# Banded attention and a feed-forward on one core: the score products in eight pieces of 32 queries instead of four of 64

## The chip, the core and the metric

One core of one Trainium2 chip runs the whole kernel. The metric is the device time of one execution in microseconds (us); lower is better.

## The reference

Four batches, eight heads, 768 positions, head dimension 64. Each query sees the 8 global keys and the 96 latest positions with itself; scores carry a per-head linear bias by distance. The attention output, 3072 tokens of 512, then goes through a gated feed-forward without activation.

```python
scores = scale * np.matmul(q, k.transpose(0, 1, 3, 2))
keep = is_global | ((rel >= 0) & (rel < n_local))        # 8 global, 96 local
scores = np.where(keep, scores + bias, -1e9)
a = softmax(scores)
x = np.matmul(a, v)                                      # then (B*S, H*D)
out = ((x @ w1) * (x @ w2) @ w3) @ w_out
```

## The kernel before, in words

Queries are worked in chunks of 256 (`T`), twelve chunks in all (`NC`), three per batch. A chunk has four pairs of heads (`NP`); a step `s` takes two pairs of one chunk, so there are 24 steps. The two heads `u` of a pair lie on the two halves of the partitions (rows 0 to 63 and 64 to 127), so a product of one head contracts 64 rows.

`scores(c, hp, qr)` (from L408) makes the scores of one pair of heads. For each of the two blocks `j` of 128 queries, for each half `g` of 64 queries (`HQ`) and each head `u`, one matmul (L419) takes 64 queries as weights and streams the keys that these 64 queries can see: 96 window keys, 8 global keys and the own ones, cut to columns g*64 to g*64+167 of the 232 (`UW`), 168 columns. Its output stands on 64 of the 128 partitions of a PSUM bank; each head `u` has a bank of its own (`ps[u]`). So four products (two halves by two heads) sit on four different 64x64 quarters of the array. The first block of a batch has no window before it (`w0 = BW` cuts the first 104 columns): its halves stream 64 and 128 columns. The data are plain float32; the profile has two matmul and two weight-load records for each such product.

`rows` (L434, L435) takes the scores from PSUM: VectorE adds the bias and finds the maximum, ScalarE exponentiates. `values` (L522) makes attention times V, also in 64x64 quarters (rows 64 or 40, 64 columns of weights, 64 or 128 columns streamed). The probabilities come back transposed through DRAM (`swap`, L484; `back`, L493) and are used two steps later.

The order of TensorE's work is written out by hand. From step 5 on, `visit(s, sv, True)` issues for step `s`: the scores of the first pair, half of the products of `values` of step s-2, the scores of the second pair, the other half of `values`. Then `slices` issues a run of the feed-forward (L172 to L174, L192 to L194: 128x128 weights, 512 or 256 streamed columns, in a one-pass float32 format), 72 matmuls long, until the next visit. Steps 0 to 3 (`first_visit`) issue half of `values`, both scores, the other half, between matmuls that fold w3 and w_out (L153); step 0 has no `values`, and step 4 has scores alone. After the 24 steps come two visits of `values` alone (128 or 104 rows of weights, 64 columns) and the rest of the feed-forward.

Of the kernel before, what the change touches and what calls it, by code (L numbers as in the profile page):

```python
# [20 lines left out]
P = 128  # L21
# [7 lines left out]
BK = 32  # L29
NB = P // BK  # L30
# [3 lines left out]
SLOT = GLB + P  # L34
KW = WIN + NQ * SLOT
BW = WIN + GLB
# [5 lines left out]
HQ = P // 2  # L42
# [296 lines left out]
def banded(ctx, tc, ff, ns, nt, nf, oki, ident, qk, vx):  # L339


    nc = tc.nc
# [64 lines left out]
    def scores(c, hp, qr):  # L407

        ps = sc[hp % STEP]
        for j in range(NQ):
            w0 = BW if c % NCB == 0 and j == 0 else 0
            for g in range(P // HQ):
                cols = slice(max(w0, g * HQ), BW + (g + 1) * HQ)
                q0 = KW + j * P + g * HQ
                for u in range(2):
                    m = qr[u * D:(u + 1) * D]
                    nc.tensor.matmul(ps[u][g * HQ:(g + 1) * HQ, j, cols], lhsT=m[:, q0:q0 + HQ], rhs=m[:, j * SLOT:][:, cols], start=True, stop=True)  # L419
        return ps  # L420

    def rows(c, hp, ps):
# [138 lines left out]
    def visit(s, sv, ahead):  # L561


        uu = None if sv is None else spread(sv)
        ps = [None, None]

        def some(i):
            ps[i] = scores(*pairs(s)[i], qrs[s][i])

        def half(k):  # L570
            if uu is not None:
                if k:
                    nc.scalar.activation(uu[:, :, T], ident[:, :STEP], AF.Copy)
                values(uu, sv, k)

        if ahead:
            some(0)
        half(0)
        if not ahead:
            some(0)  # L580
        some(1)
        half(1)
        return ps, uu
# [157 lines left out]
    with tc.manual_schedule(engines={mybir.EngineType.PE}):  # L741
        with tc.manual_schedule(engines={mybir.EngineType.DVE, mybir.EngineType.SP}):
            first_steps()
        with tc.manual_schedule(engines={mybir.EngineType.Activation, mybir.EngineType.SP}):
            for s in range(SWAP + 1, n):
                sv = s - 2 if s > SWAP + 1 else None
                ps, uu = visit(s, sv, True)
# [66 lines left out]
```

## Time and profile before

| | |
|---|---|
| median of 3 runs | 553.4 us (550.91 to 554.24) |
| the profiled execution, its own time | 552.61 us |
| its span in the trace | 550.8 us (1.8 us lie around it) |
| TensorE (PE) busy | 529.9 us, 96% of the span |
| VectorE, ScalarE busy | 308.8 us, 241.7 us |
| matmul records | 4232, of which L419 has 768 and L522 1376 |
| granted TensorE clock, mean | 0.994 |

The profile is of one execution. A matmul's record has its start; its end is modelled, so the time that one takes from the next is read from the distance of two starts and not from its duration. The merged timeline puts neighbouring instructions of one line and operation into one row with their count; the row's shape is that of the first of them. A short window of the timeline shows the instructions that lie in it, so the first start in such a row tells one group of matmuls from the next.

### The profile page before, as it was taken

The page shows a single profiled execution, that of the slowest core. Times are in us where ns is not written, and L with a number is a line of the kernel's source. Part 1 is how long each engine was busy: PE and PEld are TensorE (multiplying, and loading weights), DVE is VectorE, ACT ScalarE, POOL GpSimd, SP SyncE. Part 2 cuts the span into 40 slices and gives each one's busy share as a digit, 9 for nine tenths or more (in the row PEclk, how much of TensorE's full clock was granted, in tenths as well). Part 3 has the DMA queues.
Part 4 walks back from the last instruction along what each step waited for, and adds up shares of the span by engine and source line. Part 5 has one row for each costly group of instructions (what it writes and reads, how often), then busy time and mean ns, then how long its engine had stood idle before and what let it go on. Part 6 is the DMA issues. An engine that isn't in the chain of part 4 may idle for free.

```text
span 550.8 us, 10912 instructions
## 1 busy us (share of the span) xinstructions
PE 529.9 (96%) x4232; PEld 422.5 (77%) x4232; DVE 308.8 (56%) x930; ACT 241.7 (44%) x713; POOL 4.7 (1%) x22
## 2 busy tenths in 40 slices
PE   2999999999898999999999999999999999999995
PEld 0445559989886888888888888888888888888884
DVE  8999999976575457525655544565266551023200
ACT  3065687565465346415643553454265341122210
POOL 0000000000000000000000000000000000000000
PEclk9999999999899999999999999999999999999998
DMA  8897556769999676478547765864784475100011
GB/s 294 308 355 286 192 206 239 200 228 260 228 234 252 164 221 167 147 205 242 135 145 194 187 210 150 231 142 149 225 236 137 126 202 129 52 1 0 0 40 43
DMA packets 47420, 98.64 MB, mean 179 GB/s; under 512 B 3968, under 2 KB 27520, under 8 KB 47360
## 3 DMA queue, kind: packets, MB, share of 16 engines
q1 hardware_dynamic: 47360, 97.86, 59.7%
q8 instruction: 35, 0.57, 0.4%
q14 instruction: 25, 0.20, 0.1%
HBM read 69.54 MB, written 28.31 MB: 178 GB/s over the span
## 4 chain that ended last, share of the span: by engine, by line
PE 86%; DMA 7%; DVE 2%; ACT 2%; SPq 1%; issue 1%; DVEq 0%; ACTq 0%
PE m L172 15%; PE m L174 15%; PE m L173 15%; PE w L153 9%; PE o L192 8%; PE o L193 7%; PE o L194 7%; PE v L522 5%; PE s L419 5%; DMA ph<-d 5%; DMA stage<-w3t 1%; DMA d<-ph 1%; SPq L493 1%; ACT pr L435 1%; DVE pr L434 1%
## 5 line engine op out<-in xcount | busy, mean ns | idle before, releaser
L435 ACT ACTIVATE pr<-pr,mx 128x232 f32<-128x232 f32 (+1 forms) x192 | 88.1, 461 | 26.6 <-DVE mx L434 26.3
L172 PE MATMUL m<-xh,w2h 128*128 128x512 f32 (+1 forms) x224 | 82.1, 367 | 0.0
L181 DVE TENSOR_TENSOR a<-m,a 128x512 f32<-128x512 f32 x48 | 32.9, 685 | 85.8 <-PE m L174 85.6
L173 PE MATMUL m<-xl,w2h 128*128 128x512 f32 (+1 forms) x224 | 80.9, 361 | 0.0
L174 PE MATMUL m<-xh,w2l 128*128 128x512 f32 (+1 forms) x224 | 80.7, 360 | 0.0
L172 PE MATMUL m<-xh,w1h 128*128 128x512 f32 (+1 forms) x224 | 80.6, 360 | 0.0
L174 PE MATMUL m<-xh,w1l 128*128 128x512 f32 (+1 forms) x224 | 80.4, 359 | 0.0
L173 PE MATMUL m<-xl,w1h 128*128 128x512 f32 (+1 forms) x224 | 80.3, 359 | 0.0
L192 PE MATMUL o<-wh,gh 128*128 128x512 f32 x192 | 76.0, 396 | 0.0
L64 ACT ACTIVATE gh<-a 128x512 fp32r<-128x512 f32 x45 | 28.4, 632 | 106.8 <-DVE a L181 106.8
L434 DVE CUSTOM_DVE_ANT_0 pr<-s,biasw 128x232 f32<-128x232 f32 x160 | 53.7, 395 | 38.2 <-PE s L419 38.2
L193 PE MATMUL o<-wl,gh 128*128 128x512 f32 x192 | 74.9, 390 | 0.0
L194 PE MATMUL o<-wh,gl 128*128 128x512 f32 x192 | 74.7, 389 | 0.0
L484 DVE STREAM_TRANSPOSE ph<-pr 128x512 f32<-128x512 f32 x84 | 49.2, 642 | 2.8 <-ACT pr L447 2.3
L153 PE MATMUL w<-wo,t 128*128 128x512 f32 x80 | 39.9, 633 | 9.4 <-DVE wo L59 9.4
L172 PEld LDWEIGHTS m<-xh,w2h 128*128 128x128 f32 x224 | 42.7, 191 | 7.1 <-DVE oki L335 0.2
L174 PEld LDWEIGHTS m<-xh,w2l 128*128 128x128 f32 x224 | 42.7, 191 | 6.4
L179 ACT ACTIVATE a<-m 128x512 f32<-128x512 f32 x48 | 28.5, 593 | 43.5 <-PE m L174 43.5
L173 PEld LDWEIGHTS m<-xl,w2h 128*128 128x128 f32 x224 | 42.7, 191 | 6.0
L172 PEld LDWEIGHTS m<-xh,w1h 128*128 128x128 f32 x224 | 42.3, 189 | 6.4
L174 PEld LDWEIGHTS m<-xh,w1l 128*128 128x128 f32 x224 | 42.3, 189 | 6.4
L173 PEld LDWEIGHTS m<-xl,w1h 128*128 128x128 f32 x224 | 42.3, 189 | 6.3
(93 smaller groups left out, 664.2 us busy)
## 6 DMA issues: line engine op xcount, KB each, us to landing
d<-ph SPq DMA_DIRECT2D x42, 512.0 KB, 5.8
ph<-d SPq DMA_DIRECT2D x84, 256.0 KB, 7.9
qr<-qk SPq DMA_DIRECT2D x16, 624.0 KB, 4.1
vr<-vx SPq DMA_DIRECT2D x17, 512.0 KB, 6.1
stage<-w3t SPq DMA_DIRECT2D x15, 512.0 KB, 6.3
out_dram<-ot SPq DMA_DIRECT2D x24, 256.0 KB, 4.3
raws<-w SPq DMA_DIRECT2D x10, 512.0 KB, 6.2
qr<-qk SPq DMA_DIRECT2D x8, 520.0 KB, 4.6
```

Of the source, the lines that this page charges most:

```text
L153: nc.tensor.matmul(ps, lhsT=self.t3[f, z][:, i * P:(i + 1) * P].bitcast(F32), rhs=self.wo[:, k].bitcast(F32), start=k == 0, stop=k == NFC - 1)
L172: nc.tensor.matmul(ps[:, z], lhsT=mh, rhs=xh[:, i], start=i == 0, stop=False)
L173: nc.tensor.matmul(ps[:, z], lhsT=mh, rhs=xl[:, i], start=False, stop=False)
L174: nc.tensor.matmul(ps[:, z], lhsT=ml, rhs=xh[:, i], start=False, stop=i == NCC - 1)
L179: nc.scalar.activation(a, ps, AF.Copy)
L181: nc.vector.tensor_tensor(out=a, in0=ps, in1=a, op=ALU.mult)
L192: nc.tensor.matmul(ps, lhsT=gh[:, f, ts], rhs=self.wh[:, f], start=f == 0, stop=False)
L193: nc.tensor.matmul(ps, lhsT=gh[:, f, ts], rhs=self.wl[:, f], start=False, stop=False)
L194: nc.tensor.matmul(ps, lhsT=gl[:, f, ts], rhs=self.wh[:, f], start=False, stop=f == NFC - 1)
L434: nc.vector.tensor_tensor_reduce(out=pr[:, j, u, w0:], in0=ps[u][:, j, w0:UW], in1=bias, scale=-SCALE, scalar=3.0e38, op0=ALU.add, op1=ALU ...
L435: nc.scalar.activation(pr[:, j, u, w0:], pr[:, j, u, w0:], AF.Exp, bias=m, scale=-1.0, accum_out=sm[:, j, u:u + 1])
L484: nc.vector.transpose(x[:, k, :, u1 - 4 + u0:u1], units[:, u0:, k0:k0 + P].rearrange("p u (b c) -> p b u c", c=BK))
```

## The change

In `scores` the loop over halves of 64 queries becomes a loop over blocks of 32 queries (`NB` = 4, `BK` = 32). Each product has 32 columns of weights and streams the columns g*32 to g*32+135, 136 of them; in the first block of a batch 32, 64, 96 and 128 columns. The eight products of a block (four blocks by two heads) stand on eight different 64x32 pieces of the array. `values` stays in 64x64 quarters, the feed-forward in the whole array. Nothing else is edited.

```diff
@@ -411,12 +411,12 @@
         ps = sc[hp % STEP]
         for j in range(NQ):
             w0 = BW if c % NCB == 0 and j == 0 else 0
-            for g in range(P // HQ):
-                cols = slice(max(w0, g * HQ), BW + (g + 1) * HQ)
-                q0 = KW + j * P + g * HQ
+            for g in range(NB):
+                rows, q0 = slice(g * BK, (g + 1) * BK), KW + j * P + g * BK
+                cols = slice(max(w0, g * BK), BW + (g + 1) * BK)
                 for u in range(2):
                     m = qr[u * D:(u + 1) * D]
-                    nc.tensor.matmul(ps[u][g * HQ:(g + 1) * HQ, j, cols], lhsT=m[:, q0:q0 + HQ], rhs=m[:, j * SLOT:][:, cols], start=True, stop=True)
+                    nc.tensor.matmul(ps[u][rows, j, cols], lhsT=m[:, q0:q0 + BK], rhs=m[:, j * SLOT:][:, cols], start=True, stop=True)
         return ps
```

On TensorE, in the visit of step 16 (s_103 and s_104 are the banks of the two heads of the first pair, v the output of `values`, o the feed-forward's last product), before:

```order
L194 MATMUL o_0_3187<-wh,gl_2744 128x512
L419 MATMUL s_103<-qr_0_3081 64x168
L419 MATMUL s_104<-qr_0_3081 64x168
L419 MATMUL s_103<-qr_0_3081 64x168
L419 MATMUL s_104<-qr_0_3081 64x168
L419 MATMUL s_103<-qr_0_3081 64x168
L419 MATMUL s_104<-qr_0_3081 64x168
L419 MATMUL s_103<-qr_0_3081 64x168
L419 MATMUL s_104<-qr_0_3081 64x168
L522 MATMUL v_0_3200<-ph_0_2928,vr_0_3083 64x128 x4
```

The same place after, from the second block (j = 1) of the first pair on; eight rows like the first eight stand ahead of it:

```order
L419 MATMUL s_103<-qr_0_3337 32x136
L419 MATMUL s_104<-qr_0_3337 32x136
L419 MATMUL s_103<-qr_0_3337 32x136
L419 MATMUL s_104<-qr_0_3337 32x136
L419 MATMUL s_103<-qr_0_3337 32x136
L419 MATMUL s_104<-qr_0_3337 32x136
L419 MATMUL s_103<-qr_0_3337 32x136
L419 MATMUL s_104<-qr_0_3337 32x136
L522 MATMUL v_0_3456<-ph_0_3168,vr_0_3339 64x128 x4
L522 MATMUL v_0_3456<-ph_0_3168,vr_0_3339 64x64 x4
```

Four products of a block became eight, and the products of `values` that follow them are as they were.

On TensorE, in the visit of step 12, the scores of a batch's first block, before:

```order
L419 MATMUL s_103<-qr_0_2317 64x64
L419 MATMUL s_104<-qr_0_2317 64x64
L419 MATMUL s_103<-qr_0_2317 64x128
L419 MATMUL s_104<-qr_0_2317 64x128
L419 MATMUL s_103<-qr_0_2317 64x168
L419 MATMUL s_104<-qr_0_2317 64x168
```

And after:

```order
L419 MATMUL s_103<-qr_0_2509 32x32
L419 MATMUL s_104<-qr_0_2509 32x32
L419 MATMUL s_103<-qr_0_2509 32x64
L419 MATMUL s_104<-qr_0_2509 32x64
L419 MATMUL s_103<-qr_0_2509 32x96
L419 MATMUL s_104<-qr_0_2509 32x96
L419 MATMUL s_103<-qr_0_2509 32x128
L419 MATMUL s_104<-qr_0_2509 32x128
L419 MATMUL s_103<-qr_0_2509 32x136
```

The longest product of the first block streams 128 columns in both; the others became shorter. On VectorE, ScalarE, GpSimd and SyncE the instructions stand in the order in which they stood.

## Rows read from the trace of the kernel before

**Rows 1.** From the page: the share that each engine is busy (first row), then for TensorE the busy tenths in 40 slices of the span, and the granted TensorE clock in tenths.

```profile
PE 529.9 (96%) x4232; PEld 422.5 (77%) x4232; DVE 308.8 (56%) x930; ACT 241.7 (44%) x713; POOL 4.7 (1%) x22
PE   2999999999898999999999999999999999999995
PEclk9999999999899999999999999999999999999998
```

**Rows 2.** From the page: the chain that ended last, shares of the span by engine.

```profile
PE 86%; DMA 7%; DVE 2%; ACT 2%; SPq 1%; issue 1%; DVEq 0%; ACTq 0%
```

**Rows 3.** Busy time by stage: the stretch, its length, the busy time of PE, PEld, DVE, ACT and POOL with the number of instructions, the granted clock, the DMA share and GB/s.

```profile
25.00:84.00 59.00, 58.73 (x440) 31.01 (x433) 57.21 (x152) 37.23 (x107) 0.00 (x0) 1.00 0.70 250
116.00:176.00 60.00, 55.66 (x720) 50.35 (x720) 37.69 (x146) 33.85 (x117) 1.14 (x4) 0.97 0.92 248
250.00:400.00 150.00, 150.00 (x1254) 124.38 (x1256) 77.15 (x249) 67.50 (x206) 1.13 (x4) 1.00 0.66 184
```

**Rows 4.** TensorE's timeline over the visit of step 16: start in us, time to the last modelled end, line, operation, tiles, shape, count.

```profile
302.60 0.39 PE L193 MATMUL o<-wl,gh 128*128 128x512 f32 x1
302.83 0.39 PE L194 MATMUL o<-wh,gl 128*128 128x512 f32 x1
303.15 0.80 PE L419 MATMUL s<-qr 64*64 64x168 f32 x16
303.77 0.85 PE L522 MATMUL v<-ph,vr 64*64 64x128 f32 x32
304.44 0.76 PE L419 MATMUL s<-qr 64*64 64x168 f32 x16
305.01 0.86 PE L522 MATMUL v<-ph,vr 64*64 64x128 f32 x32
305.80 0.50 PE L192 MATMUL o<-wh,gh 128*128 128x512 f32 x1
306.13 0.40 PE L193 MATMUL o<-wl,gh 128*128 128x512 f32 x1
306.37 0.39 PE L194 MATMUL o<-wh,gl 128*128 128x512 f32 x1
```

**Rows 5.** The same timeline in short windows inside that visit: the first group of four score matmuls (its first one alone, then all four), the second, third and fourth group by the first start of each row, then the last two groups of four 64-column matmuls of `values`.

```profile
303.15 0.35 PE L419 MATMUL s<-qr 64*64 64x168 f32 x1
303.15 0.37 PE L419 MATMUL s<-qr 64*64 64x168 f32 x4
...
303.34 0.61 PE L419 MATMUL s<-qr 64*64 64x168 f32 x12
303.48 0.47 PE L419 MATMUL s<-qr 64*64 64x168 f32 x8
303.62 0.32 PE L419 MATMUL s<-qr 64*64 64x168 f32 x4
...
305.56 0.31 PE L522 MATMUL v<-ph,vr 64*64 64x64 f32 x8
305.62 0.25 PE L522 MATMUL v<-ph,vr 64*64 64x64 f32 x4
```

**Rows 6.** TensorE's timeline at the visit with `values` alone (step 22's values, 128 rows by 64 columns of weights): the matmul ahead of it, the first three groups by the first start of each row, the last group, and the two matmuls behind it.

```profile
455.77 0.39 PE L194 MATMUL o<-wh,gl 128*128 128x512 f32 x1
456.09 0.55 PE L522 MATMUL v<-ph,vr 128*64 128x128 f32 x6
456.25 0.39 PE L522 MATMUL v<-ph,vr 128*64 128x128 f32 x4
456.36 0.39 PE L522 MATMUL v<-ph,vr 128*64 128x128 f32 x4
...
457.79 0.28 PE L522 MATMUL v<-ph,vr 104*64 104x128 f32 x2
458.00 0.50 PE L192 MATMUL o<-wh,gh 128*128 128x512 f32 x1
458.33 0.40 PE L193 MATMUL o<-wl,gh 128*128 128x512 f32 x1
```

**Rows 7.** The timeline of the weight loads (PEld) at the visit of step 16; in brackets the idle time before a row.

```profile
302.61 0.19 PEld L194 LDWEIGHTS o<-wh,gl 128*128 128x128 f32 x1
303.14 0.49 PEld L419 LDWEIGHTS s<-qr 64*64 64x64 f32 x16 [0.35 <-issue]
```

**Rows 8.** Length and busy time of six visits, columns as in Rows 3: steps 0, 3, 4, 16, 12 (scores of a batch's first block) and 14 (values of a batch's first block).

```profile
24.80:25.97 1.17, 1.17 (x34) 0.93 (x33) 1.17 (x4) 0.00 (x0) 0.00 (x0) 1.00 0.22 39
81.46:84.11 2.65, 2.65 (x98) 2.58 (x97) 2.56 (x6) 1.51 (x4) 0.00 (x0) 1.00 0.00 0
104.88:106.18 1.30, 1.30 (x33) 1.06 (x32) 1.23 (x10) 0.60 (x1) 0.00 (x0) 1.00 1.07 212
303.15:305.80 2.65, 2.65 (x98) 2.56 (x97) 1.80 (x11) 1.12 (x6) 0.00 (x0) 1.00 0.03 6
226.97:229.49 2.52, 2.52 (x97) 2.37 (x96) 1.73 (x13) 1.05 (x6) 0.00 (x0) 1.00 0.02 7
265.19:267.60 2.41, 2.41 (x85) 2.31 (x85) 1.56 (x9) 1.59 (x6) 0.00 (x0) 1.00 0.00 0
```

**Rows 9.** TensorE's timeline in the stretch in which it waits for the probabilities' way through DRAM (steps 6 and 8).

```profile
141.20 0.44 PE L522 MATMUL v<-ph,vr 64*64 64x128 f32 x4 [0.22 <-DMA ph<-d]
143.12 0.77 PE L522 MATMUL v<-ph,vr 40*64 40x128 f32 x24 [1.49 <-DMA ph<-d]
...
170.38 0.61 PE L522 MATMUL v<-ph,vr 64*64 64x64 f32 x18 [1.13 <-DMA ph<-d]
```

## The prediction

> **What bounds the kernel now.** I read the page's shares first, then the chain that ended last, then the stages, and then single visits of the timeline. TensorE is busy 96% of the span, and its busy tenths stand at 9 from the second slice nearly to the end; the clock row shows full speed in all slices but one and the last [rows 1]. The chain runs over TensorE for 86% [rows 2]. In the long middle, 250 to 400 us, TensorE is busy 150.00 of 150 us [rows 3]: there, what a visit takes longer or shorter moves the end by as much. Only between 116 and 176 us does it wait, for 4.3 us in all [rows 3].
>
> One visit is the unit of everything below. That of step 16 reads [rows 4]: the last feed-forward matmul starts at 302.83, the first scores at 303.15, values at 303.77, second scores at 304.44, values at 305.01, feed-forward again at 305.80. So a pair's scores take 0.62 and 0.57 us, and the visit 2.65 us [rows 8].
>
> **What streaming costs.** The score matmuls start in groups of four, at 303.15, 303.34, 303.48, 303.62, with values at 303.77 [rows 5, 4]: a pass of 168 columns takes 0.1425 us, and a pair's scores are four passes (two blocks, two records for each product), 0.57 us. Four products are therefore in flight together, since 16 records of 0.14 us in a row would be 2.3 us. A pass of 128 columns takes 0.109 us (456.25 to 456.36 [rows 6]), one of 64 columns 0.056 to 0.06 us (305.56 to 305.62 [rows 5]). Between the first two that is 0.84 ns a column, so 136 columns take 0.109 + 8 x 0.00084 = 0.116 us, if eight products run together as four do now. A pair's scores then stream 4 x 0.116 = 0.463 us: 0.107 us less. In a batch's first block the longest products stream 128 columns and 136 after it, 2 x 0.109 + 2 x 0.116 = 0.45 us against 0.109 x 2 + 0.1425 x 2 = 0.50: 0.05 less. There are 48 pairs, 16 of them with a first block: 32 x 0.107 + 16 x 0.053 = 4.3 us. That is all that the change can bring.
>
> The issue rate seems not to stand against it: the four starts of a group lie within 0.37 - 0.35 = 0.02 us, 7 ns apart [rows 5], so eight start within 0.047 us, less than one pass; and 64-column passes already issue four matmuls and four loads in 0.056 us, 14 ns a pair, which is what eight in 0.116 us need.
>
> **What a change of the array's cut costs.** Feed-forward matmuls start 0.227 us apart (302.60, 302.83), but the first scores start 0.32 us after the last of them: 0.09 us lost [rows 4]. The weight loads show why: the next load could have come one matmul earlier, but starts at 303.14, beside its own matmul, after 0.35 us of idle "issue" [rows 7]. The array runs dry before it is cut anew, and the first load is in the open: the first pass takes 0.19 us instead of 0.1425, 0.05 more for 64 columns of weights. On the way out, the last group starts at 305.62 [rows 5]; the last of its four starts 0.03 later and ends its pass at 305.71; the feed-forward starts at 305.80, again 0.09 later, and its next start is 0.33 behind instead of 0.227: 0.10 more for 128 columns of weights. The visit with 128x64 weights shows the same two prices: 455.77 to 456.09, then 0.16 for the first pass against 0.11; and 457.79 + 0.109 to 458.00, then 0.33 [rows 6]. Between scores and values, both in 64x64 quarters, there is no such loss now (304.44 + 0.57 = 305.01 [rows 4]).
>
> After the change scores stand in 64x32 pieces and values in 64x64 quarters, so a visit has three more changes of cut: scores to values, values to scores, scores to values. No row shows a change between these two cuts. The bounds: 0 at the least, and at the most what 64x64 to 128x128 costs, 0.09 + 0.10 + 0.03 of skew = 0.22 us. The nearest rows are those into 64-wide weights, 0.09 + 0.05; for 32-wide weights I take half the open load, 0.025 us, since 64 cost 0.05 and 128 cost 0.10. I take 0.09 dry, plus 0.05 or 0.025, plus the skew of the last group, since a dry array waits for the last piece: 0.03 for values, 0.047 for eight scores.
>
> The Trainium skill bears on the open point: "TensorEngine Tiling (Array Packing)", Key Properties, says that changing the tiling mode, unlike changing the tile, drains the engine. The trace agrees where the whole array is one side (the 0.09 us above), and no row here shows it between two small cuts. Another of its pages, "TensorE: Matmul & The Clock Gate", Part 3, gives about 4 ns for each further tile; the rows have 7 ns, and the rows decide: by the page the skew of eight would be 0.028 instead of 0.047, about 1 us less over 48 pairs.
>
> **The sum, against the profiled execution (552.6 us; span 550.8).** Visit of step 16: three dry ends +0.28; open loads +0.05 + 0.05 (values), +0.025 (second scores), -0.025 (first scores, 32 wide now) = +0.10; skew 2 x 0.047 + 0.03 = +0.12; streaming -0.21. Together +0.28, 2.65 to 2.93 us. Seven visits are like it (steps 5, 10, 11, 16, 17, 22, 23): +2.0.
>
> Visits whose scores have a first block (6, 7, 12, 13, 18, 19) take 2.52 [rows 8]. Today a quarter that is done early goes on with values; after the change all wait for the 128-column piece. Scores 0.45 + 0.025 + 0.047 + 0.09 = 0.61 each, values 0.67 + 0.05 + 0.02 + 0.09 = 0.83 and 0.79 + 0.04 = 0.83: 2.88, +0.37 each, +2.2 for six. Visits whose values have a first block (8, 9, 14, 15, 20, 21) take 2.41 [rows 8]: 2 x 0.625 for scores, 0.61 and 0.72 for the shorter values make 2.58; with the lags that the present 2.41 also has, between +0.17 and +0.28, I take +0.22: +1.3.
>
> Early steps: step 0 (1.17 us) and step 4 (1.30 us [rows 8]) have two pairs' scores and no values, so no new change of cut: -0.10 and -0.21. Steps 1 to 3 (step 3: 2.65 us [rows 8]) have two new ones against two pairs' saving: +0.1 to +0.2 each, +0.5. Together +0.2. Between 25 and 84 us VectorE is nearly as full (57.21 of 59 us [rows 3]), so this may come out smaller.
>
> In steps 6 to 8 the first values wait for a transfer anyway (1.49 and 1.13 us [rows 9]) and hide the change ahead of them: -0.4. The later ones of these visits are not hidden: loads of the next step go out when the visit has ended.
>
> Sum: 2.0 + 2.2 + 1.3 + 0.2 - 0.4 = 5.3, rounded to 5.5 us for lags as in the last kind of visit. 552.6 + 5.5 = 558.1; the median of the runs shown is 0.8 above the profiled one, so 558.9: I say 559.0 us. VectorE and ScalarE see scores 0.05 earlier or 0.2 later; they wait for TensorE at these points now and have room.
>
> **The rivals.**
> *A. No dry array between the two small cuts.* Pieces of 64x32 would follow quarters of 64x64 as quarters follow one another now. For it: inside a visit nothing is lost between scores and values today, quarters run ahead of one another. Against it: every change of cut that the trace shows is paid, even into 128x64. Then the full 4.3 us come back: 553.4 - 4.3 = 549.1. It decides below 4.3 us over 63 new changes (19 x 3 + 3 x 2), 0.07 us each; from there the change is no longer slower.
> *B. Still only four products at a time.* Eight pieces need four streams of keys from the same 64 partitions instead of two, and no row shows four. If they share what two have, or if two pieces take turns in a quarter, a pair's scores take 8 passes of 0.116, 0.93 us against 0.57: +0.36 x 48 = +17 us, 570 without dry ends and 576 with them. For it: only that the rate of four streams is unseen. Against it: today four loads and four matmuls overlap in two streams a half without loss [rows 5].
> *C. The wait that lowered the clock.* In one slice the granted clock falls [rows 1], in the stage with the 1.49 us wait (mean 0.97 over 60 us [rows 3]), worth 1.8 us. It may come or go with a small shift: +-1.8 us on any case.
>
> **How the numbers follow.** Forecast 0.68 (556 to 563), A 0.18 (547.5 to 551), B 0.14 (568 to 578). A measurement here can tell about 1% from no change, 5.5 us: the forecast's centre lies on that line, so half of it counts as slower (0.36 with its upper tail) and the rest as the same; B is slower; A is within 1% in two of three cases. Slower 0.50, same 0.44, faster 0.06. The range from 549 to 566 leaves out most of B and the lower part of A.
>
> **What would show it.** In the visit of step 16, now at about the same place: score passes of eight starts within 0.05 us, 0.116 us apart (right), or two sets of four (B). Gaps between scores and values: the first values pass 0.05 long, and a start about 0.09 after the last score pass has streamed; PEld idle "issue" not once but four times a visit. Visit length 2.9 us. If it is 2.45 us, A holds; at 3.3 or more, B. L419 shows 1536 matmul records. I am wrong if visits grow and the end does not, or if the difference lies outside the visits.

## The result and the profile after

The changed kernel takes 559.48 us (median of 4, 558.77 to 561.05), the kernel before 553.12 in the runs beside it: ratio 1.0124, 95% interval 1.0085 to 1.0163. The forecast was 559.0. The profiled execution took 559.07 us, its span is 557.3 us, 6.5 more than before.

The busy row of [rows 1] and the row of [rows 2], of the kernel after:

```profile
PE 535.3 (96%) x5000; PEld 419.3 (75%) x5000; DVE 309.8 (56%) x930; ACT 241.6 (43%) x713; POOL 4.7 (1%) x22
PE 86%; DMA 7%; DVE 2%; ACT 2%; SPq 1%; issue 1%; DVEq 0%; ACTq 0%
```

TensorE has 768 more matmul records (1536 of L419 instead of 768) and is busy 5.4 us longer; VectorE and ScalarE are within 1 us of before. Below, "matmuls" with a count are such records, two to a product. The chain runs over it as before.

TensorE's timeline over the visit of step 16, to be laid beside [rows 4]:

```profile
307.05 0.39 PE L194 MATMUL o<-wh,gl 128*128 128x512 f32 x1
307.37 0.69 PE L419 MATMUL s<-qr 64*32 64x136 f32 x32
307.99 0.90 PE L522 MATMUL v<-ph,vr 64*64 64x128 f32 x32
308.82 0.69 PE L419 MATMUL s<-qr 64*32 64x136 f32 x32
309.45 0.90 PE L522 MATMUL v<-ph,vr 40*64 40x128 f32 x32
310.27 0.50 PE L192 MATMUL o<-wh,gh 128*128 128x512 f32 x1
```

From one start to the next: scores 0.62, values 0.83, scores 0.63, values 0.82 us. Values, which nobody edited, were 0.67 and 0.79; the scores, which were to become shorter, are as long as before (0.62) or longer (0.57). Short windows of the same timeline show why, as in [rows 5]: the first of the eight score matmuls and all eight, then the second, third and fourth pass by the first start of each row, then the first two passes of values, the last pass of values and the scores behind it.

```profile
307.37 0.30 PE L419 MATMUL s<-qr 64*32 64x136 f32 x1
307.37 0.35 PE L419 MATMUL s<-qr 64*32 64x136 f32 x8
307.50 0.53 PE L419 MATMUL s<-qr 64*32 64x136 f32 x20
307.62 0.44 PE L419 MATMUL s<-qr 64*32 64x136 f32 x16
307.74 0.32 PE L419 MATMUL s<-qr 64*32 64x136 f32 x8
...
307.99 0.34 PE L522 MATMUL v<-ph,vr 64*64 64x128 f32 x4
308.15 0.41 PE L522 MATMUL v<-ph,vr 64*64 64x128 f32 x12
...
308.65 0.24 PE L522 MATMUL v<-ph,vr 64*64 64x64 f32 x4
308.82 0.33 PE L419 MATMUL s<-qr 64*32 64x136 f32 x6
```

Eight products do run together: eight starts lie within 0.35 - 0.30 = 0.05 us, and the passes follow 0.12 us apart (307.50, 307.62, 307.74). The scores' last pass starts at 307.74, its eighth matmul 0.05 later, and has streamed at 307.74 + 0.05 + 0.116 = 307.90; values start at 307.99, 0.09 later. Their first pass takes 0.16 us (308.15 - 307.99) where 0.109 is usual: 0.05 for loads in the open. The last values start from 308.65 on, 0.06 of pass and 0.03 of skew end at 308.74, and the scores start at 308.82, 0.08 later. The weight loads show the same from their side: the idle "issue" of [rows 7] now also stands ahead of both blocks of values. Ahead of the second scores the loads pause only 0.06 us (307.99 + 0.77 to 308.82), so the view marks three such pauses in the visit, not the four that were to be seen.

```profile
307.36 0.41 PEld L419 LDWEIGHTS s<-qr 64*32 64x32 f32 x32 [0.35 <-issue]
307.99 0.77 PEld L522 LDWEIGHTS v<-ph,vr 64*64 64x64 f32 x32 [0.21 <-issue]
308.82 0.41 PEld L419 LDWEIGHTS s<-qr 64*32 64x32 f32 x32
309.44 0.76 PEld L522 LDWEIGHTS v<-ph,vr 40*64 40x64 f32 x32 [0.21 <-issue]
```

The six visits of [rows 8], in the same order (steps 0, 3, 4, 16, 12, 14):

```profile
24.92:26.00 1.08, 1.08 (x65) 0.87 (x64) 1.08 (x4) 0.00 (x0) 0.00 (x0) 1.00 0.18 19
81.64:84.43 2.79, 2.79 (x130) 2.44 (x129) 2.69 (x6) 1.63 (x4) 0.00 (x0) 1.00 0.02 6
105.09:106.24 1.15, 1.15 (x65) 0.94 (x65) 1.08 (x9) 0.60 (x1) 0.00 (x0) 1.00 1.12 219
307.37:310.27 2.90, 2.90 (x129) 2.35 (x128) 2.03 (x13) 1.31 (x6) 0.00 (x0) 1.00 0.02 6
230.02:232.90 2.88, 2.88 (x129) 2.32 (x128) 1.88 (x13) 1.30 (x7) 0.00 (x0) 1.00 0.02 6
268.89:271.56 2.67, 2.67 (x118) 2.11 (x117) 1.89 (x11) 1.80 (x7) 0.00 (x0) 1.00 0.02 6
```

Where no change of cut was added (steps 0 and 4) the visit is shorter by 0.09 and 0.15 us, although its products doubled; everywhere else it is longer, by 0.14 (step 3), 0.25, 0.36 and 0.26. The 14 visits from step 10 on make 6 x 0.26 + 4 x 0.36 + 4 x 0.26 = 4.0 us (by the starts the visit of step 16 takes 2.905 us, 0.26 more). That is what lies between the start of step 10 (188.59 us before, 191.10 after, the next two rows, the first of before) and the end of the span: 362.2 us before, 366.2 after.

```profile
188.59 0.37 PE L419 MATMUL s<-qr 64*64 64x168 f32 x4
```

```profile
191.10 0.35 PE L419 MATMUL s<-qr 64*32 64x136 f32 x8
```

The other 2.5 us came up before step 10; more on them below.

### The profile page after: what moved, and what is told of

Same layout as the page of the kernel before. It is cut to its first block, busy times and chain, and to the rows that moved or that the text cites. A ratio compares the mean times of both kernels' runs of the same rounds, so it can differ in the third digit from the quotient of the medians.

```text
span 557.3 us, 12448 instructions
## 1 busy us (share of the span) xinstructions
PE 535.3 (96%) x5000; PEld 419.3 (75%) x5000; DVE 309.8 (56%) x930; ACT 241.6 (43%) x713; POOL 4.7 (1%) x22
## 4 chain that ended last, share of the span: by engine, by line
PE 86%; DMA 7%; DVE 2%; ACT 2%; SPq 1%; issue 1%; DVEq 0%; ACTq 0%
PE m L172 15%; PE m L174 14%; PE m L173 14%; PE w L153 8%; PE o L192 7%; PE o L193 7%; PE o L194 7%; PE v L522 7%; PE s L419 5%; DMA ph<-d 5%; DMA d<-ph 2%; DMA stage<-w3t 1%; SPq L493 1%; ACT pr L435 1%; ACT pr L447 1%
```

## The experiments

The theory on trial, D: each change between the 64x32 and the 64x64 cut lets the array run dry and opens the first load. The rival, I: the loss sits in the eighths themselves, in the issue of twice as many products. The table gives the times (n executions, the ratio against the kernel before in the runs beside them) and the length of three visits, taken from the starts in each timeline; it is these that tell the theories apart, since TensorE waits for no other engine in them, but for one wait named below. These lengths are within 0.01 us in two traces of one kernel, while the time scatters: the kernel before took between 550.6 and 557.8 us.

| run | n | median us | ratio, 95% | step 16 | step 12 | step 14 |
|---|---|---|---|---|---|---|
| before, in four sets of runs | 4 to 25 | 552.25 to 553.81 | | 2.65 | 2.52 | 2.41 |
| changed | 4 | 559.48 | 1.0124 (1.0085 to 1.0163) | 2.91 | 2.88 | 2.67 |
| changed, again | 6 | 560.41 | 1.0140 (1.0094 to 1.0187) | 2.91 | 2.88 | 2.67 |
| changed, values first | 10 | 560.31 | 1.0109 (1.0078 to 1.0140) | 2.81 | 2.74 | 2.58 |
| before, values first | 10 | 556.11 | 1.0046 (1.0016 to 1.0077) | 2.65 | 2.51 | 2.41 |
| changed, finer | 4 | 576.44 | 1.0456 (1.0407 to 1.0504) | 3.55 | 3.52 | 3.52 |
| before, finer | 4 | 562.11 | 1.0170 (1.0126 to 1.0213) | 2.88 | 2.81 | 2.70 |
| values in eighths too | 10 | 557.71 | 1.0083 (1.0056 to 1.0110) | 2.85 | 2.78 | 2.44 |
| values in eighths only | 4 | 570.43 | 1.0299 (1.0241 to 1.0357) | 3.42 | 3.29 | 3.03 |
| changed, values first from step 10 | 4 | 559.74 | 1.0122 (1.0079 to 1.0165) | 2.81 | 2.74 | 2.58 |
| the same, again | 12 | 558.69 | 1.0094 (1.0067 to 1.0122) | 2.81 | 2.74 | 2.58 |
| before, last two visits cut up | 1 | 558.51 | | 2.65 | 2.52 | 2.41 |

**One change of cut less.** The order within a visit, from step 5 on, once on the changed kernel and once on the kernel before:

```diff
-                ps, uu = visit(s, sv, True)
+                ps, uu = visit(s, sv, False)
```

> The changed kernel (64x32 scores), but from step 5 on a visit issues half of the values, both pairs' scores, the other half: two new changes of cut a visit instead of three. Theory D (the array runs dry at each change of cut and the first load is in the open): one dry end (0.09), one open load (0.05) and one skew (0.02 to 0.05) less, visit of step 16 about 2.75 us instead of 2.91, 19 visits, about 3 us faster than the changed kernel: 556.5 us, ratio to the kernel before 1.006. Rival I (the loss is in the eighths themselves: issue, loads, skew within a pass): the number of changes does not matter, the time stays at 559.5, ratio 1.012.

> Control: the kernel before (64x64 scores) in the same order, half of the values, both pairs' scores, the other half. No change of cut within a visit in either order. Both theories: visit 2.65 us, time as before, 553 us within 0.3%; if the order itself brings something (a later start of the scores, an earlier need of the probabilities), it is seen here and is taken off the other run.

In the visit the change of cut shows, 0.09 to 0.14 us less for one change, while the control's visits stay within 0.01 us. It is not the whole 0.16 that theory D had: both pairs' scores now stand in one block of 64 matmuls, and that block is 0.06 longer than two of 32 without their dry end (rows below, 310.40 to 311.55).

```profile
310.40 1.22 PE L419 MATMUL s<-qr 64*32 64x136 f32 x64
311.55 0.90 PE L522 MATMUL v<-ph,vr 40*64 40x128 f32 x32
```

But the time did not fall, and the control rose by 2.7 us (556.11 against 553.46), which neither theory had. From step 10 to the end the control's trace is as long as before (362.5 and 362.2 us), so its loss lies ahead of that. The waits view shows part of it: TensorE's waits for the probabilities (`ph<-d`), in total us, times and the longest, of the kernel before (two rows; the second is a wait of the same matmuls in step 9 that the view puts down to VectorE) and of the control.

```profile
PE v L522 <- DMA ph<-d: 3.0, 4, 1.5
PE v L522 <- DVE mx L434: 1.3, 1, 1.3
```

```profile
PE v L522 <- DMA ph<-d: 6.6, 5, 1.8
```

So 4.3 us became 6.6 us. The granted clock over the same stage, 116 to 188 us, is 0.95 instead of 0.98 too, worth up to 0.03 x 72 = 2.2 us. Values stand first in the visit there, and no scores cover the transfer in steps 6 to 9; that this made the waits longer is likely, but one trace of each does not show it.

**The order changed from step 10 alone.**

```diff
-                ps, uu = visit(s, sv, True)
+                ps, uu = visit(s, sv, s < 10)
```

> The changed kernel; from step 10 on alone a visit issues half of the values, both pairs' scores, the other half (two new changes of cut instead of three); steps 5 to 9, which wait for the transfer of the probabilities, stay as they are. Theory D: 0.16 us less in each of 14 visits, 2.3 us: 557.2 us, ratio 1.007. Rival W (the order put the first values ahead of the scores that covered the transfer, and this cost 2.5 us in the earlier pair of runs): the same 557.2 here, since that stage is left alone. If it stays at 559.5 or above, the order costs elsewhere too.

> The changed kernel once more, beside the next one on the same chip, to have both over more executions. Theory D: 559.5 us, ratio to the kernel before 1.012; visits from step 10 on as in its first trace (2.91, 2.88 and 2.67 us), whatever steps 5 to 9 do.

> The changed kernel with half of the values ahead of both pairs' scores from step 10 on, once more. In its first trace the 14 visits from step 10 on were 1.5 us shorter in all than the changed kernel's, while steps 5 to 9, the same program in both, came out 2.6 us later. If those 2.6 us are the scatter of single executions (waits and the granted clock in that stage), the median here lies 1.5 us under the changed kernel's beside it, about 558.0 us; if the order costs something in every execution, both medians are equal again.

The first try came out at 559.74, no gain, though its 14 visits were 6 x 0.10 + 4 x 0.14 + 4 x 0.09 = 1.5 us shorter. Its step 10 started at 193.73 us, the changed kernel's at 191.10, with the same program up to there. The waits do not account for that (4.3 us for `ph<-d` against 5.0). The granted clock does: 0.93 instead of 0.98 from 116 to 188 us, worth up to 0.05 x 72 = 3.6 us; from 133.1 to 136.3 and from 160.4 to 167.0 us it stood at 0.50, the lower of its two levels (1.2 instead of 2.4 GHz), beside waits of 1.6 and 2.0 us, and in the changed kernel only once so, behind the wait in step 9. The two stretches, of the changed kernel and of this run (columns as in [rows 3]):

```profile
116.00:188.00 72.00, 66.85 (x922) 57.50 (x922) 42.63 (x155) 37.34 (x124) 1.13 (x4) 0.98 0.89 245
```

```profile
116.00:188.00 72.00, 67.28 (x913) 57.58 (x912) 42.70 (x155) 36.86 (x123) 1.28 (x4) 0.93 0.88 232
```

The repeat, beside the changed kernel on one chip, gave 558.69 against 560.41: 1.7 us less, the size that the visits have. Single executions scatter by more than that, and the two intervals in the table overlap; what shows the gain without scatter is the part from the start of step 10 to the end, 364.8 and 364.7 us in the two traces of this order, 366.2 and 366.3 in the two of the changed kernel. So the scatter of the stage ahead of step 10 had hidden it.

**Twice as many changes of cut.** The same products, alternating by block and by quarter of the values (the new order; `scores` and `values` were given a choice of the block and of the quarter, which is left out here):

```diff
+    def finer_visit(s, sv):
+        uu, ps = spread(sv), [None, None]
+        for k in range(2):
+            for j in range(NQ):
+                ps[k] = scores(*pairs(s)[k], qrs[s][k], (j,))
+                if k and not j:
+                    nc.scalar.activation(uu[:, :, T], ident[:, :STEP], AF.Copy)
+                values(uu, sv, k, bool(j))
```

> The changed kernel with the same products, but from step 5 on a visit alternates twice as often: scores of one block, a quarter of the values, and so on: seven new changes of cut a visit instead of three. Theory D: in the changed kernel's trace a block of scores is 0.160 us longer than its passes and a block of values 0.171 us; two more of each a visit are +0.66 us, 19 visits: 559.5 + 12.6 = 572 us, visit of step 16 about 3.57 us. Rival I (the loss lies in the eighths, not in the change of cut): 559.5 us.

> Control: the kernel before in the same finer alternation; scores and values stand in the same 64x64 quarters, so no change of cut within a visit. Both theories: visit 2.65 us, 553.5 us within 0.4%. If alternating by itself costs, it is seen here.

The visit of step 16 of the changed kernel in the finer order, the first two of its eight blocks and the end:

```profile
315.55 0.46 PE L419 MATMUL s<-qr 64*32 64x136 f32 x16
315.95 0.56 PE L525 MATMUL v<-ph,vr 64*64 64x128 f32 x16
...
319.10 0.50 PE L192 MATMUL o<-wh,gh 128*128 128x512 f32 x1
```

3.55 us against the 3.57 that theory D had; four more changes cost 0.64 us, 0.16 each, with not one product more. It is 0.64 in the visit of step 12 too, but 0.85 in that of step 14, of which 0.2 stays unexplained. The control's visit was to stay at 2.65 and became 2.88. That is one wait: between the two halves of the values stands a ScalarE copy that orders them, and in the finer order only one block of scores covers it (the weight loads, with the wait in brackets):

```profile
311.75 0.32 PEld L525 LDWEIGHTS v<-ph,vr 40*64 40x64 f32 x12 [0.31 <-ACT v L594]
```

In the changed kernel in this order that copy is hidden behind the dry ends (all four gaps in the weight loads ahead of values are alike there, 0.21 us), so its 0.64 is the price of the changes and not of this wait. The control's span rose 8.9 us, its visits 5.1 of them; the rest lies in steps 6 to 9 again (it waits 7.5 us for `ph<-d`). The changed kernel's span rose 14.0 us in the profiled execution, its visits 13.4 of them; that execution is the fastest of four (573.08 us), and no trace shows where the median's 3.4 us more went.

**No change of cut within a visit.** Values, but for the two last visits, are cut to 32 columns of V too: in the changed kernel, where scores and values then stand in the same pieces, and, as the reverse, in the kernel before, where three changes of cut a visit come in (`...` stands for what is as it was):

```diff
-            nc.tensor.matmul(uu[u * D:(u + 1) * D, ...], lhsT=v[r], ...)
+            w = D if k == 2 else BK
+            for d in range(0, D, w):
+                nc.tensor.matmul(uu[u * D + d:u * D + d + w, ...], lhsT=v[r][:, d:d + w], ...)
```

> The changed kernel, and values' products (except the two last visits) are cut into 32 columns of V as well, so that scores and values stand in the same 64x32 pieces: no change of cut within a visit, twice as many products of values. Theory D: the four passes of a pair's scores stay at 0.463 us, values stream as before, nothing is lost between them: visit 2.40 to 2.45 us, about 4.5 us faster than before, 548.7 us, ratio 0.992. Rival I: eight pieces with 64-column passes need a pair of load and matmul every 7 ns and cannot be issued so; values take longer than 0.67 us and the time is above 559.5.

> The kernel before with 64x64 scores, and only values' products cut into 64x32 pieces: three changes of cut a visit as in the changed kernel, without what the eighths save in the scores. Theory D: three dry ends 0.27, open loads 0.10, skew 0.11 us a visit, visit of step 16 about 3.12 us, with the early steps about 9.5 us slower than before: 562.6 us, ratio 1.017. Rival I: no loss by the change of cut, 553 us, unless 64-column passes of eight can't be issued in 0.056 us, which would show inside values.

Both theories lose something. With all in eighths (step 22's visit):

```profile
421.88 0.69 PE L419 MATMUL s<-qr 64*32 64x136 f32 x32
422.37 0.95 PE L524 MATMUL v<-ph,vr 64*32 64x128 f32 x55
...
423.71 1.08 PE L524 MATMUL v<-ph,vr 40*32 40x128 f32 x64
424.73 0.50 PE L172 MATMUL m<-xh,w2h 128*128 128x512 f32 x1
```

The scores take 0.49 us now, 0.13 less than in the changed kernel, and values follow without a gap: the dry end is gone where the cut does not change, as D says. But values, 64 matmuls instead of 32, take 1.02 us behind the second scores where 0.79 was usual, and the visit ends at 2.85 us, not at 2.40. The visit of step 14, with 48 and 56 matmuls of values instead of 64 and 64, comes to 2.44, near the 2.41 of before. With values alone in eighths the visit is 3.42 us, 0.30 above D's 3.12, by the same lengthening. So three changes of cut and the supply of many small matmuls are two costs, and the second shows only in runs of more than 32 matmuls: the 32 of a score block in the changed kernel kept their pace.

The time of 557.71 us holds a third thing. In steps 5 to 8 TensorE stands still four times, about 4 us in all, within or shortly behind these visits, and waits for nothing that the profile shows; the kernel before has no such row in its waits view. The longest, of this run:

```profile
PE m L172 <- issue: 2.0, 1, 2.0
```

**The supply by itself.** In the kernel before, only in the two last visits (values alone), each product is cut into four of 32 streamed columns. In the first of the two the weights keep their 64 columns (two pieces of 128x64), in the second they are cut to 32 as well (four pieces of 128x32). Of the edit, the two cuts:

```diff
+                    if k == 2:
+                        cut = [(q, BK) for q in range(0, P, BK)]
...
+            w = BK if k == 2 and s == NC * NP // STEP - 1 else D
```

> The kernel before; only in the two last visits of values alone each product is cut into four of 32 streamed columns: in the first with 64 columns of weights (two pieces of 128x64), in the second with 32 columns of weights as well (four pieces of 128x32). A 32-column pass streams in 0.028 us. Theory P (a load and its matmul together take 13 ns to issue, however small): the first passes every 0.028 us for two pieces (14 ns a pair), the second every 0.053 us for four. Theory L (the load of a piece's weights bounds, 0.05 us for 64 columns, 0.027 for 32): the first every 0.053 us for two pieces, the second every 0.028 us for four, 7 ns a pair.

The starts of two passes of the first visit, of two passes of the second, and the second's whole run:

```profile
457.72 0.40 PE L526 MATMUL v<-ph,vr 128*64 128x32 f32 x8
457.78 0.40 PE L526 MATMUL v<-ph,vr 128*64 128x32 f32 x8
...
478.31 0.38 PE L526 MATMUL v<-ph,vr 128*32 128x32 f32 x24
478.35 0.38 PE L526 MATMUL v<-ph,vr 128*32 128x32 f32 x24
...
477.86 1.60 PE L526 MATMUL v<-ph,vr 128*32 128x32 f32 x164
481.40 1.00 PE L526 MATMUL v<-ph,vr 128*32 128x32 f32 x92 [1.94 <-issue]
```

Two pieces with 64 columns of weights need 0.06 us a pass (128 matmuls in 3.7 us: 0.058), four with 32 columns need 0.033, though both stream 32 columns. So the pass follows the width of the load, as theory L has it (0.053 and 0.028), and there is no floor of 13 ns for a load and its matmul: theory P, which had it the other way round, fell. After 164 matmuls at 8 ns each the engine then stood still for 1.94 us, again with nothing to wait for that the profile shows.

## Why the prediction was right

*Streaming.* A pass of 136 columns was put at 0.116 us; the starts give 0.12, and in steps 0 and 4, without new changes of cut, 0.10 and 0.21 us were to be gained and 0.09 and 0.15 were. Rival B (four at a time) fell with the eight starts in 0.05 us.

*The change of cut.* The one price that no row showed was taken from the nearest rows: 0.09 dry, 0.05 or 0.025 for open loads, 0.03 to 0.05 of skew. The trace gives 0.08 to 0.09 dry and 0.05 open; score and value blocks of the visit came out at 0.62, 0.83, 0.63, 0.82 where 0.625, 0.83, 0.625, 0.83 were put. Rival A fell in the trace, and by experiment in both directions: four changes more cost 0.64 us in visits like that of step 16, one less gave back 0.09 to 0.14. The Trainium skill, "TensorEngine Tiling (Array Packing)", Key Properties, says that changing the mode drains the engine; the trace now shows it between two small cuts as well, 0.09 us.

*The sum by visits.* Like step 16 +0.28, measured +0.26; first blocks +0.37, measured +0.36; values of a first block +0.22, measured +0.26. From step 10 on, 14 visits: 6 x 0.28 + 4 x 0.37 + 4 x 0.22 = 4.0 put, 4.0 measured. That the sums are equal is luck in part: the first two kinds were put 0.01 to 0.02 too high, the third 0.04 too low. The +0.22 had been lifted from a worked-out 0.17 by a guess at lags; the guess was in the right direction. (Three dry ends of 0.09 make 0.27, not the 0.28 put down for them; the sum of +0.28 is that with 0.27.)

*Where the sum was off.* Before step 10 it had +1.5 us (1.3 for steps 0 to 9 and 0.2 of rounding), and the profiled executions differ by 2.5. Visits 0 to 5 explain 0.4, steps 6 to 9 the other 2.1. The term that failed is the -0.4 for a change of cut hidden behind waits. It rested on [rows 9], which are of steps 7 and 9, not 6 and 8: in the trace before, steps 6 and 8 hardly wait. In the trace after, all four steps wait, 5.2 us in all (the next row and 0.2 more) where 4.3 were (the 3.0 and 1.3 above). The granted clock from 116 to 188 us is 0.98 in both, so rival C plays no part between these two. That leaves 1.2 us, and the lengthening that these kinds of visit have from step 10 on is 2 x 0.36 + 2 x 0.26 = 1.2: nothing of it was hidden.

```profile
PE v L522 <- DMA ph<-d: 5.0, 4, 1.7
```

That the change made the waits longer is not shown. The run with the last two visits cut up has the program of the kernel before through step 23, and waits 5.9 us in these steps; four traces have the changed program up to step 10 and wait 5.2, 7.4, 4.6 and 4.2 us. Step 10 starts at 188.59 and 190.00 us in the former two, at 191.10, 192.27, 193.73 and 191.98 in the latter four: later every time, by 3.0 us on average, of which the visits make 1.6. The rest can be the scatter of this stage, which comes from the waits and, as the 193.73 shows, from the clock.

That 559.0 came within 0.5 us of 559.48 is therefore luck in part: the profiled execution is 6.5 us longer where 5.5 was put, and the median of the runs lies 0.4 above it where 0.8 was put.

The forecast's centre lay on the line of 1% and the measured 1.24% lies above it; the repeat gave 1.40%, with the interval's lower end at 0.94%.

## What to carry to other kernels

Count the changes of cut in the order in which TensorE is issued, and set 0.16 us for each against what the shorter streams save; here 63 changes, some 10 us, stood against 4.3 us. Smaller pieces of the array paid only in the two visits where no change of cut came with them (0.09 and 0.15 us). A change of cut can be priced before it is made, from the gap and the long first pass at a border that the trace already has. And look at the neighbour's rows: the loss of this edit stood partly in lines that it did not touch.

## What the runs showed of the hardware

A change between 64x32 pieces and 64x64 quarters cost 0.16 us here: 0.08 to 0.09 us in which nothing streams, the first loads in the open, and the skew of the last group of starts.

A run of more than 32 small matmuls in eight pieces was not fed at its pace. In the run with values in eighths only, 64 of them with passes of 128 and 64 columns took 0.98 us (first block of values of step 16, 313.64 to 314.62, a change of cut with it), where the passes stream in 0.66. The last row is a stretch of line 524 alone (busy time and count of PE and PEld, then the clock and DMA): 31 of the 64 start within the first 0.34 us, about their pace; the other 33 and the change of cut take 0.64.

```profile
313.64 1.05 PE L524 MATMUL v<-ph,vr 64*32 64x128 f32 x64
314.62 0.80 PE L419 MATMUL s<-qr 64*64 64x168 f32 x16
...
313.63:313.98 0.35, 0.34 (x31) 0.34 (x33) 1.00 0.00 0
```

In four pieces of 128x32 the same engine kept 8 ns a matmul over 164 of them, and then stood 1.94 us. What feeds it, why eight pieces are fed more slowly than four, and why it stands still after long runs of small matmuls (about 4 us with all in eighths, 2.0 with values in eighths only), these runs do not tell. No kernel here beats the one before: with all changes within a visit gone the supply and the standstills take back what they cost, and with one of three gone 1% is still missing.
